# A 64x32 factorization of the row transform, with real and imaginary parts stacked on the partitions and unsummed filter products, in a spectral filter beside a gated linear unit

## The chip, the cores and the metric

The kernel runs on one core of a Trainium2 chip. The metric is device time in microseconds (us) of one execution; the profile's span, from a profiled execution, is some 2 us shorter. All runs quoted here are fast ones. Before took 206.78 us when the prediction was made (median of 3 runs, 206.33 to 206.89), and 206.92 to 206.98 in the three rounds of experiments (medians of 7 to 11 runs, 206.16 to 207.72).

## The reference

The output is the sum of the input, a two-dimensional spectral filter of its layer norm, and a gated product of the same layer norm.

```python
xn = (x - mean(x)) / sqrt(var(x) + 1e-5)             # x: 2048 x 640, bf16
X  = rfft2(xn, axes=(-2, -1))                        # 2048 x 321, complex
ya = irfft2(X * (w_r + 1j * w_i), s=(2048, 640))     # w_r, w_i: 2048 x 321
yb = ((xn @ w_gate) * (xn @ w_up)) @ w_down          # 640 x 1536, 1536 x 640
out = x + ya + yb
```

## The kernel before

A planner runs when the kernel is built. It knows every task, an estimated duration on each engine that may do it, and the buffers, and fixes the order of instructions on every engine. "First products" below means the matmuls with w_gate and w_up. The planner uses them, 512 columns wide, to fill TensorE while a spectral task waits for another engine.

The spectral stage goes through 16 iterations, each a chain over engines: column transform D (TensorE), its copy out of PSUM (ScalarE or VectorE), row transform C (TensorE), filter product WM (VectorE), sums CB (GpSimd), negations NG (ScalarE), inverse transform IA (TensorE). The planner keeps several iterations in flight. The filter rows come by one transfer for each of two halves of 64 partitions, w_r and w_i apart.

```python
for t in range(16):
    for w_ in range(2):                       # w_r, w_i
        for h in range(2):                    # two halves of 64 partitions
            dma(v_w[64 * h:64 * h + 64, wr, w_, 0:321], wvs[w_][:, k2, :])
    # D: 5 matmuls, real and imaginary columns side by side
    for k in range(5):
        n = 128 if k < 4 else 130
        matmul(psum[:, ...k * 128 + n], v_uq[:, k, t, :], v_fd[:, k * 128: k * 128 + n])
    # C: complex product as 4 real matmuls for two row groups
    matmul(ps[:, bk, 0:_LP],     v_tf[:, t, 0, :], a_r, start=True,  stop=False)
    matmul(ps[:, bk + 1, 0:_LP], v_tf[:, t, 0, :], a_i, start=True,  stop=False)
    matmul(ps[:, bk, 0:_LP],     v_tf[:, t, 1, :], a_i, start=False, stop=True)
    matmul(ps[:, bk + 1, 0:_LP], v_tf[:, t, 2, :], a_r, start=False, stop=True)
    # WM (VectorE): four products x * w.  ... CB (GpSimd): their sums, NG (ScalarE): negated copies ...
    # IA: 5 pairs of 128 columns; weights l1, l2 are read with a step of 4 for k < 4
    for k in range(5):
        matmul(dst, l1, v_ti[:, t, 0, :], start=True,  stop=False)
        matmul(dst, l2, v_ti[:, t, 1, :], start=False, stop=True)
```

## Time and profile before

| | before |
|---|---|
| time, span | 206.78 us, 204.3 us |
| TensorE busy | 98%, granted clock 1.00 throughout |
| VectorE, ScalarE, GpSimd busy | 87%, 59%, 11% |
| spacing of matmuls from start to start | 216 ns (512 columns), 137 (320 or 321), 56 (128) |
| first real product starts at | 7.57 us |

How to read it: TensorE has work from beginning to end, so the sum of its matmuls is the time, nearly. The other engines and the transfers count only where they let TensorE run dry. The prediction shows the views that carry this. One view is added here because the result turns on it: busy time in the stretch from 84 to 141 us, which is the spectral stage (columns: stretch, length, busy time of PE, PEld, DVE, ACT and POOL with instruction counts, granted clock, mean busy share of the 16 DMA engines, GB/s).

```profile
84.00:141.00 57.00, 56.30 (x478) 36.35 (x486) 44.95 (x144) 48.82 (x126) 21.56 (x32) 1.00 0.30 67
```

TensorE is idle for 0.7 of 57 us here, and the transfers bring 67 GB/s without anyone waiting for them.

### The profile page before, as it was taken

What the parts mean: (1) busy time and instruction counts of PE and PEld (TensorE: products, weight loads), DVE (VectorE), ACT (ScalarE), POOL (GpSimd) and SP (SyncE); (2) the same over time, 40 slices, a digit from 0 to 9 for tenths busy, and PEclk for the clock granted to TensorE, in tenths of its full rate; (3) what the DMA queues carried; (4) which work ended last, traced back from release to release, by engine and by line L of the source; (5) the groups of instructions that cost most, each with busy time, mean ns of one, the idle gap of its engine ahead of it and who ended that gap; (6) DMA issues with size and microseconds to landing.
All of it is one profiled execution on the core that took longest, in us unless ns stands there. A gap on an engine that the chain in (4) does not pass through costs nothing.

```text
span 204.3 us, 4499 instructions
## 1 busy us (share of the span) xinstructions
PE 199.7 (98%) x1681; PEld 137.2 (67%) x1695; DVE 178.7 (87%) x508; ACT 121.4 (59%) x282; POOL 21.8 (11%) x36
## 2 busy tenths in 40 slices
PE   7999999999999999999999999999999999999995
PEld 7998999554545455465777666666777787777774
DVE  3798999999999999949997997818999999999973
ACT  2379998999976577577999899878420222000000
POOL 0000000000000000003655365310000000000000
PEclk9999999999999999999999999999999999999999
DMA  6999993603139460001333343225033122324212
GB/s 179 301 342 383 387 210 15 67 0 64 32 66 242 86 202 0 3 0 27 66 65 60 68 113 65 65 70 158 0 98 113 55 76 83 112 80 111 83 35 62
DMA packets 30740, 21.69 MB, mean 106 GB/s; under 512 B 10752, under 2 KB 29696, under 8 KB 30592
## 3 DMA queue, kind: packets, MB, share of 16 engines
q1 hardware_dynamic: 29920, 21.06, 40.6%
q10 hardware_dynamic: 800, 0.36, 0.6%
q8 instruction: 13, 0.21, 0.4%
q14 instruction: 7, 0.06, 0.1%
HBM read 16.82 MB, written 2.62 MB: 95 GB/s over the span
## 4 chain that ended last, share of the span: by engine, by line
PE 92%; DVE 6%; issue 1%; ACT 1%
PE ps L969 36%; PE ps L1229 26%; PE ps L989 13%; DVE arena L1070 3%; PE ps L747 3%; PE ps L930 2%; PE ps L1146 2%; PE ps L1239 2%; PE ps L1034 2%; PE ps L1117 2%; PE ps L1118 2%; DVE arena L1073 1%; PE ps L1058 1%; PE ps L1055 1%; PE ps L1057 1%; PE ps L1056 1%
## 5 line engine op out<-in xcount | busy, mean ns | idle before, releaser
L719 ACT ACTIVATE arena<-ps 128x512 bf16<-128x512 f32 (+5 forms) x183 | 97.1, 568 | 48.7 <-PE ps L1146 23.4
L969 PE MATMUL ps<-arena 128*128 128x512 bf16 x346 | 80.1, 379 | 0.9 <-DVE arena L1073 0.3
L969 PEld LDWEIGHTS ps<-arena 128*128 128x128 bf16 x360 | 33.9, 98 | 36.5 <-ACT arena L719 0.8
L1229 PE MATMUL ps<-arena 128*128 128x320 bf16 (+2 forms) x396 | 56.7, 295 | 0.0
L1229 PEld LDWEIGHTS ps<-arena 128*128 128x128 bf16 x396 | 38.0, 98 | 13.9
L989 PE MATMUL ps<-arena 128*128 128x128 bf16 (+1 forms) x360 | 28.2, 237 | 0.1
L989 PEld LDWEIGHTS ps<-arena 128*128 128x128 bf16 x360 | 24.9, 98 | 2.5 <-ACT arena L719 0.7
L1070 DVE TENSOR_TENSOR arena<-ps,arena 128x256 f32<-128x256 f32 x64 | 22.6, 414 | 1.4 <-PE ps L1058 1.2
L1005 DVE TENSOR_TENSOR arena<-arena 128x512 bf16<-128x512 bf16 x36 | 15.3, 425 | 9.0 <-ACT arena L719 8.8
L1093 POOL TENSOR_TENSOR arena<-arena 128x256 bf16<-128x256 f32 x16 | 10.3, 644 | 111.5 <-DVE arena L1086 111.5
L1249 DVE TENSOR_TENSOR arena<-ps,arena 128x320 bf16<-128x320 f32 (+2 forms) x33 | 15.3, 473 | 3.8 <-PE ps L1239 3.8
L1094 POOL TENSOR_TENSOR arena<-arena 128x256 bf16<-128x256 f32 x16 | 11.9, 745 | 0.0
L1117 PE MATMUL ps<-arena 128*128 128x128 bf16 x80 | 10.4, 219 | 0.1
L1118 PE MATMUL ps<-arena 128*128 128x128 bf16 x80 | 10.4, 219 | 0.0
L1117 PEld LDWEIGHTS ps<-arena 128*128 128x128 bf16 x80 | 8.7, 111 | 1.7
L1118 PEld LDWEIGHTS ps<-arena 128*128 128x128 bf16 x80 | 8.7, 112 | 1.4
L1239 PE MATMUL ps<-arena 128*128 128x320 bf16 (+2 forms) x33 | 9.1, 295 | 0.0
L883 DVE TENSOR_TENSOR arena<-arena 128x384 f32<-128x384 bf16 x16 | 8.8, 551 | 0.0
L773 ACT ACTIVATE arena<-arena 128x640 bf16<-128x640 bf16 x10 | 8.3, 825 | 0.0
L782 DVE BATCH_NORM_STATS2 arena<-arena 128x6 f32<-128x320 bf16 x12 | 5.4, 481 | 2.8 <-DMA arena<-in_A_x_dram 2.7
L767 ACT ACTIVATE arena<-arena 128x640 bf16<-128x640 bf16 x10 | 7.3, 734 | 0.3 <-DMA arena<-in_A_x_dram 0.2
L1073 DVE TENSOR_TENSOR arena<-ps,arena 128x260 f32<-128x260 f32 x16 | 7.0, 438 | 0.0
(72 smaller groups left out, 235.7 us busy)
## 6 DMA issues: line engine op xcount, KB each, us to landing
arena<-in_A_x_dram SPq DMA_DIRECT2D x20, 160.0 KB, 2.5
out_dram<-arena SPq DMA_DIRECT2D x31, 80.0 KB, 1.6
arena<-c_tf SPq DMA_DIRECT2D x4, 384.0 KB, 11.2
arena<-in_A_w_r_dram SPq DMA_DIRECT2D x32, 40.1 KB, 2.3
arena<-in_A_w_i_dram SPq DMA_DIRECT2D x32, 40.1 KB, 2.3
arena<-in_B_w_gate_dram SPq DMA_DIRECT2D x4, 320.0 KB, 5.4
arena<-in_A_x_dram SPq DMA_DIRECT2D x1, 1280.0 KB, 10.3
arena<-c_ti SPq DMA_DIRECT2D x2, 512.0 KB, 4.9
```

What stands on the lines that cost most here:

```text
L719: return c.e.activation(dst, src, _ACTF.Copy)
L969: ins = c.e.matmul(ps[:, bk, :], v_gw[:, w, j, ft, :], v_xt[:, j, rows], start=(j == 0), stop=(j == 4))
L989: ins = c.e.matmul(ps[:, bk, w * n:(w + 1) * n], v_gw[:, w, j, ft, :], v_xt[:, j, rows], start=(j == 0), stop=(j == 4))
L1005: return c.e.tensor_tensor(v_ht[:, ft0, rows], v_gbf[:, rr, 0, :], v_gbf[:, rr, 1, :], _OP.mult)
L1070: c.e.tensor_tensor(v_p[:, ar, w, :, 128 * h:128 * h + 128].rearrange("p c (m k) -> p c m k", k=4), xh.rearrange("p c (m k) -> p c m k", k ...
L1093: c.e.tensor_tensor(v_y[ar][:, 512:768], p01[:, 0:256], p10[:, 0:256], _OP.add)
L1094: return c.e.tensor_tensor(v_y[ar][:, 256:512], p00[:, 0:256], p11[:, 0:256], _OP.subtract)
L1117: c.e.matmul(dst, l1, v_ti[:, t, 0, :], start=True, stop=False)
L1118: ins = c.e.matmul(dst, l2, v_ti[:, t, 1, :], start=False, stop=True)
L1229: ins = c.e.matmul(ps[:, bk, 0:sl3.stop - sl3.start], v_ht[:, ft, a * 128:(a + 1) * 128], v_wd[:, ft, sl3], start=(ft == 7 and px is None) ...
L1239: return c.e.matmul(ps[:, bank_of(own), 0:sl3.stop - sl3.start], v_sm[:, 2, :], v_v[:, a, sl3], start=False, stop=True)
L1249: return c.e.tensor_tensor(v_out[:, a % 2, sl3], ps[:, bk, 0:sl3.stop - sl3.start], v_xr[:, xs, sl3], _OP.add)
```

## The change

The intent is to save TensorE work. With the length of 2048 factored as 64 by 32, one row group has 32 points; its real and imaginary parts together fill 64 partitions, and the two sets that C multiplies fill 128. The complex product becomes one real matmul for each row group. The filter product is no longer summed: IA gets the products with w_r and with w_i as they are, and its matmul adds them up, since they lie on different partitions or in its second weight. CB falls away; a larger negation remains, on GpSimd. The filter rows are needed on four blocks of 32 partitions, two of them equal and two in reverse order of row groups, and are loaded for two iterations at once.

```diff
-_R = 32
+_R = 64
 # filter loads, one set for every two iterations, two slots
-dma(v_w[64 * h:64 * h + 64, wr, w_, 0:321], wvs[w_][:, k2, :])
+parts = [(dw[0:64], wv[:, q0:q0 + _WQ, :].rearrange("k1 q l -> k1 (q l)").unsqueeze(0).to_broadcast(
+    [2, _S1, _WQ * 321]), 64 * _WQ * 642)]
+for d_ in range(2):
+    parts.append((dw[64 + 32 * d_:96 + 32 * d_, ...], wv[:, _R - q0 - o_:_R - q0 - _WQ:-1, :], ...))
 # D: 10 matmuls of 64 or 65 columns for 5 of 128 or 130
+for w in range(2):
+    matmul(ps[:, bk + w, k * 64:k * 64 + n], v_uq[:, k, t, :], v_fd[:, k * 128 + w * n: ...])
 # C: 1 matmul for each of two row groups, for 4 in all
+for g in range(2):
+    matmul(ps[:, bk + g, 0:_LP], v_tf[:, 2 * t + g, :], v_a[:, ar, 324 * g:324 * g + _LP])
 # NG: on GpSimd, planned at 1.6 us
+tensor_scalar(yg[:, :, 0:256], yg[:, :, 512:768], -1.0, None, mult)
+tensor_copy(yg[:, :, 833:896], yg[:, :, 1025:1088])
+tensor_scalar(yg[:, :, 896:961], yg[:, :, 1024:1089], -1.0, None, mult)
+tensor_copy(yg[:, :, 961:1024], yg[:, :, 769:832])
 # IA: 20 matmuls of 64 columns for 10 of 128, output in runs of four floats
+matmul(dst[:, g], l1, v_ti[:, 2 * t + g, 0, :], start=True,  stop=False)
+matmul(dst[:, g], l2, v_ti[:, 2 * t + g, 1, :], start=False, stop=True)
 # ... tables of constants, PSUM copies, and an order retuned by the planner's parameters: cut
```

## The prediction

> **What bounds the kernel now.** I read the page's busy shares first, then the chain that ended last, then busy time by stage, then the order of matmuls inside the changed stage, and last the first nine microseconds.
>
> ```profile
> PE 199.7 (98%) x1681; PEld 137.2 (67%) x1695; DVE 178.7 (87%) x508; ACT 121.4 (59%) x282; POOL 21.8 (11%) x36
> ...
> PE 92%; DVE 6%; issue 1%; ACT 1%
> ```
>
> The first line is busy time by engine, the second the chain's shares. "Busy" for matmuls proves little, since each is drawn with its latency. So I took start-to-start spacings from the trace: 216 ns for 512 columns, 137 ns for 320 or 321, 56 ns for 128, 107 ns for 128 in the first 5 us, before the clock rises. Summed over the program's own counts (a few records are missing) they give about 200 us of the 204.3 us span. From the tenth microsecond to the last matmul I find only one real gap, 0.2 us at 118.5 us. TensorE runs out of work nowhere, and only a shorter sum of spacings, or an earlier start, can shorten the kernel. By stage (head, first products, row transforms, spectral stage, end):
>
> ```profile
> 0.00:7.60 7.60, 6.55 (x68) 6.51 (x69) 3.41 (x12) 1.87 (x3) 0.20 (x4) 1.00 0.80 219
> 7.60:36.30 28.70, 28.50 (x389) 25.96 (x388) 27.36 (x95) 25.02 (x66) 0.00 (x0) 1.00 0.97 265
> 36.30:89.00 52.70, 52.38 (x289) 26.05 (x294) 49.42 (x135) 39.75 (x79) 0.00 (x0) 1.00 0.35 74
> 89.00:142.00 53.00, 52.36 (x455) 34.22 (x462) 42.62 (x138) 46.50 (x122) 21.56 (x32) 1.00 0.32 73
> ```
>
> Columns: stretch, length, busy PE, weight loads, DVE, ACT, POOL. In the spectral stage (fourth row) DVE is busy 80% and ACT 88%: near limits, not limits. In the row stage (third row) DVE is at 94%, the closest second.
>
> **What the Trainium skill says.** "TensorE: Matmul & The Clock Gate", section "Back-to-back issue gap", gives N/2.4 + 2.5 ns for a warm stream and a floor of about 25 ns; for real streams with a weight load each it gives 81 ns at 128 columns. The trace agrees with the formula (56, 137, 216) and not with 81. No matmul of before is narrower than 128, so 64 columns, by the formula an estimate of 29.2 ns, is untested here.
>
> The same page, "Weight-path perf modes", says that full 128-column bf16 loads use a fast path that reads weights 32 bits at a time. After a wait, the trace starts a second load 15 ns behind the first, so a load is much shorter than its drawn 98 ns. But the inverse transform's weights are read with a step of four elements, and those loads are longer:
>
> ```profile
> L989 PEld LDWEIGHTS ps<-arena 128*128 128x128 bf16 x360 | 24.9, 98 | 2.5 <-ACT arena L719 0.7
> ...
> L1117 PEld LDWEIGHTS ps<-arena 128*128 128x128 bf16 x80 | 8.7, 111 | 1.7
> ```
>
> The means are 98 and 111 ns; single stepped loads show up to 117. If the 13 to 19 ns are real occupancy, a stepped load takes some 15 + 15 = 30 ns (estimate): hidden under 56 ns, just not under 29.
>
> "ScalarE: Activation LUTs", section "What ACT_TABLE_LOAD costs", states about 1283 ns for the load of a function table, again at each switch of set. The trace has one such load, 1.28 us (below).
>
> "PSUM — Partial Sum Buffer", section "Specifications (TRN2)", warns that non-contiguous access slows matmuls. The new inverse matmuls write runs of four floats, every second run. No such write is in the trace of before.
>
> **The change part by part.** It touches the column transform D, the row transform C, the filter product, the helper parts, the inverse IA; then a retuned order.
>
> TensorE. Before, D has 80 matmuls of 128 to 130 columns, C 64 of 321, IA 160 of 128: 80 x 56 + 64 x 137 + 160 x 56 ns = 4.5 + 8.8 + 9.0 = 22.2 us. After, stacking real and imaginary parts on partitions makes C one matmul per row group instead of four for two: 32 of 321 = 4.4 us. D becomes 160 of 64 or 65, IA 320 of 64: the columns streamed stay the same and the instructions double. At 29.2 ns that is 4.7 + 9.3 us. New sum 18.4 us, a gain of 3.8 us. If the 256 stepped loads hold IA at 32 ns, it costs 256 x 2.8 = 0.7 us of it, so 3.1 us are left.
>
> VectorE. Per pair of row groups, four products of 256 and one of 260 stay four of 256 and become two of 130 (by the trace's slope near 0.22 us each, for 0.36); the two subtractions of 65 (0.14 each) go. So 1.97 us becomes 1.76, 16 times: 3.3 us less. But the evacuation of D becomes four copies of 64 partitions x 321 (about 0.37 us on ACT, 0.42 on DVE, estimates from 256 and 512) for 0.86 before, and the instruction order gives 20 of the 64 to DVE: +8.3 us against some 1.7 before. DVE is up by about 3 us in the stage.
>
> ScalarE. It loses the negations (0.9 us x 16 = 14.4) and gains evacuation, 44 x 0.37 = 16.3 us for 14 x 0.8 = 11. Lighter by some 9 us.
>
> GpSimd. It swaps two f32 additions (1.37 us) for one negation of 512 elements and three pieces of 126 or 130, bf16. I guess 1.6 to 2.2 us per pair, under the 2.9 us of TensorE work per pair in the new order. None of these three lies on the path if the order holds: between a C and its IA the new order puts 4.7 to 6 us of other matmuls, and product (1.8), negation (2.2) and hand-overs (0.5) need 4.5.
>
> Head. Before:
>
> ```profile
> 1.05 5.30 PE L747 MATMUL ps<-arena 128*128 128x128 bf16 x48 [1.05 <-DVE arena L754]
> 1.70 1.28 ACT L808 ACT_TABLE_LOAD   x1 [1.70 <-PEq L1328]
> ...
> 4.59 0.21 ACT L808 ACTIVATE arena<-arena 128x1 bf16<-128x1 bf16 x1 [1.62 <-DVE arena L804]
> ...
> 5.03 0.39 DVE L826 TENSOR_SCALAR arena<-arena 128x640 bf16<-128x640 bf16 x1
> ```
>
> The first normalised tile is ready at 5.42, the warm-up ends at 6.15, the transpose follows and the first real product starts at 7.57. The change cuts 8 warm-up matmuls (0.86 us), which seems to allow 0.65 us. But it also sends tile 1's statistics to ScalarE ahead of tile 0's square root, and the built program then has two table loads: one before the first statistics pass, one before the root. The second tile lands at 3.91; 0.85 us of statistics and 1.28 of loading put the root at 6.1 for 4.59, the scaled tile at 6.9, the transpose after it, and the first product, behind VectorE's longer list, near 8.4: +0.85. Tile 1 then follows sooner (two waits of 0.42 us together, at 9.2 and 10.3, fall away). Net +0.4 us. TensorE also idles from 5.3 to 6.9, which could delay the rise of the clock: up to +0.8 more.
>
> Row stage. D now comes 7 us of TensorE work sooner (more first products are moved behind it) and DVE has only 4.7 us less to do before it. By sums of durations the last row result and the matmul that wants it are within some 0.6 us. I allow 0.5 us of stalls here and in the spectral stage.
>
> Sum: -3.8 + 0.7 + 0.4 + 0.5 = -2.2 us, 204.6; half a microsecond back for the retuned order, which was presumably measured: 204.2.
>
> **Rivals.** (1) Everything hides: 29.2 ns holds, no second load in the way, no stalls: -3.8 - 0.65 = -4.4, 202.4 us. For it: TensorE has hidden every load so far. Against: the stepped loads and the table load. (2) Narrow matmuls cost as much as wide ones, because each carries a 128-column load: 480 x 56 = 26.9 us in place of 14.0, +12.9, so about 216 us. The 15 ns between loads speaks strongly against; the unseen strided PSUM write leaves room for a part of it, say 40 ns in IA, +3.5 us. (3) VectorE or GpSimd becomes the bound of the spectral stage: DVE's list from first to last product sums to 39.5 us against 43.2 us of TensorE work, so it fits by 9% only; a GpSimd negation over 2.9 us would add (excess) x 16, for instance 3 us at 3.1.
>
> **Range and chances.** Faster by over 2% means under 202.64, which needs rival 1 nearly whole: 0.17. Slower by over 2% means over 210.9: rival 2 or a strong rival 3: 0.07. Between them 0.76. Range 202.0 to 207.2, wide to the slow side for the IA spacing, the clock and the stalls.
>
> **What would show it.** C's spacing unchanged at 137 ns with half the matmuls; D's near 29 ns; IA's 29 to 33 (over 40: rival 2 in part). A second table load around 4.8 to 6.1 us and the first product at about 8.4, not under 7. VectorE and GpSimd waits ahead of IA in the chain of waits would mean rival 3. The prediction is wrong low if gaps over 0.2 us appear before the row or inverse matmuls, and wrong high if the head starts sooner than in before and TensorE shows no gap.

## The result

The changed kernel took **228.69 us** (median of 4 runs, 226.57 to 229.67) against 206.76 of before in the same rounds: a ratio of 1.105, 95% interval 1.096 to 1.114. Slower by 10.5%, far outside the range.

The page of after, busy time, then TensorE and its granted clock in 40 slices of 5.7 us (tenths), then the chain's shares:

```profile
PE 206.1 (90%) x1900; PEld 138.8 (61%) x1917; DVE 177.3 (78%) x500; ACT 126.9 (56%) x261; POOL 40.5 (18%) x68
...
PE   7799999999999997299769579959999999999995
...
PEclk9999999999999999589979979997999999999999
...
PE 45%; DVE 22%; DMA 17%; SPq 10%; ACT 2%; issue 2%
```

TensorE, busy 98% before, is at 90%. The holes lie in slices 16 to 27, the spectral stage, and in five of the slices from 17 to 28 the clock falls to between 5 and 8 tenths, where before had none below 9. The chain, 92% TensorE before, is now 17% DMA.

Who waited for whom (engine and line that waited, what released it, us in total, times, the longest):

```profile
PEld ps L1068 <- DMA arena<-in_A_w_i_dram: 15.2, 4, 5.6
PE ps L1068 <- DMA arena<-in_A_w_i_dram: 14.0, 4, 5.1
```

L1068 is the row transform C. Four times it stands waiting for the filter load, 14.0 us in all. It waits although it reads no filter. The filter product WM frees the PSUM banks that C fills, and the planner lets C take them only once everything else that this product needs is there. So C inherits the wait for the filter.

The windows of after, with two that lie wholly inside such waits:

```profile
84.00:100.00 16.00, 10.80 (x77) 5.50 (x78) 9.54 (x27) 7.51 (x17) 7.17 (x11) 0.79 0.41 121
100.00:120.00 20.00, 16.76 (x209) 10.93 (x211) 11.56 (x34) 14.25 (x28) 9.70 (x17) 0.91 0.32 86
120.00:141.00 21.00, 16.28 (x187) 10.05 (x190) 12.38 (x38) 13.73 (x29) 11.23 (x19) 0.92 0.32 89
141.00:160.00 19.00, 16.25 (x170) 9.32 (x172) 11.59 (x35) 10.87 (x21) 12.03 (x20) 0.91 0.14 36
...
90.50:94.50 4.00, 0.00 (x0) 0.00 (x0) 2.51 (x9) 0.22 (x1) 3.47 (x5) 0.71 0.36 121
...
129.50:131.00 1.50, 0.00 (x0) 0.00 (x0) 0.06 (x1) 0.00 (x0) 1.50 (x3) 1.00 0.13 50
```

Two readings. First, the clock column: each wait is followed by stretches at half clock. Weighted by length, what is missing from full clock in these 76 us is 0.21 x 16 + 0.09 x 20 + 0.08 x 21 + 0.09 x 19 = 8.6 us, that is, 17.1 us at half clock. But 3.2 of these 17.1 us fall into the waits themselves, where TensorE has nothing to do (the row from 90.5 us shows it: no matmul, clock 0.71). TensorE worked at half clock for 13.8 us, and that took some 6.9 us more than at full clock, on top of the waits. Second, the last row: while TensorE does nothing but wait for a transfer, the 16 DMA engines are busy for 13%, two sixteenths, and move 50 GB/s. The trace has 64 packets of 2568 bytes for each load with the broadcast source, of about 104 ns each, and in this stretch 9 or 10 of them start every half microsecond. Two engines carry the whole load: 64 x 104 / 2 = 3.3 us for 160.5 KB, and w_r and w_i take 6.7 us for two iterations, whose D, C and IA and the first products planned between them hold TensorE for only 5.8.

Three smaller things are in the groups of after (line, engine, operation, shapes, count, busy us, mean ns, idle before):

```profile
L1103 POOL TENSOR_SCALAR arena<-arena 128x512 bf16<-128x512 bf16 x16 | 24.1, 1507 | 119.4 <-DVE arena L1089 119.4
...
L1122 PEld LDWEIGHTS ps<-arena 128*128 128x128 bf16 x160 | 12.8, 118 | 4.1 <-ACT arena L715 1.9
```

The large negation takes 1.5 us, and with its three small pieces GpSimd is busy for 40.5 / 16 = 2.53 us an iteration where the plan has 1.6. The weight loads of IA are drawn with 118 ns where IA of before had 111; from start to start its stepped matmuls are some 34.5 ns apart (33 to 38), those with contiguous weights 29.

The start of after, in order of time (start, length, engine, line):

```profile
5.14 1.28 ACT L804 ACT_TABLE_LOAD   x1
6.43 0.21 ACT L804 ACTIVATE arena<-arena 128x1 bf16<-128x1 bf16 x1
...
7.40 0.69 PE L840 MATMUL ps<-arena 128*128 128x128 bf16 x5 [1.91 <-DVE arena L822]
...
9.82 0.68 PE L988 MATMUL ps<-arena 128*128 128x128 bf16 x6
```

The second table load is where the prediction put it, and TensorE stands idle for 1.91 us ahead of its first transpose. The first real product starts at 9.82 us. The 36 filling matmuls between run at half clock, 53 ns each.

### The profile page after: what moved, and what is told of

Read it like the earlier page. It is cut to its first block, busy times and chain, and to the rows that moved or that the text cites. A ratio compares the mean times of both kernels' runs of the same rounds, so it can differ in the third digit from the quotient of the medians. Undisturbed runs are those within 1.5% of the kernel's fastest.

```text
span 227.9 us, 4935 instructions
## 1 busy us (share of the span) xinstructions
PE 206.1 (90%) x1900; PEld 138.8 (61%) x1917; DVE 177.3 (78%) x500; ACT 126.9 (56%) x261; POOL 40.5 (18%) x68
## 4 chain that ended last, share of the span: by engine, by line
PE 45%; DVE 22%; DMA 17%; SPq 10%; ACT 2%; issue 2%
PE ps L1234 23%; DMA arena<-in_A_w_i_dram 16%; SPq L709 10%; PE ps L968 8%; PE ps L988 5%; DVE arena L882 2%; DVE arena L1004 2%; PE ps L1244 2%; DVE arena L1086 2%; DVE arena L893 2%; DVE arena L883 1%; PE ps L1068 1%; PE ps L1151 1%; DMA arena<-in_A_x_dram 1%; DVE arena L1005 1%
## 5 line engine op out<-in xcount | busy, mean ns | idle before, releaser
L715 ACT ACTIVATE arena<-ps 128x512 bf16<-128x512 f32 (+5 forms) x203 | 106.9, 561 | 67.9 <-PE ps L968 30.2
L968 PEld LDWEIGHTS ps<-arena 128*128 128x128 bf16 x360 | 34.9, 101 | 39.7 <-issue 5.5
L1234 PE MATMUL ps<-arena 128*128 128x320 bf16 (+2 forms) x396 | 55.8, 295 | 0.0
L1234 PEld LDWEIGHTS ps<-arena 128*128 128x128 bf16 x396 | 37.7, 98 | 13.9 <-DVE arena L1254 0.3
L1103 POOL TENSOR_SCALAR arena<-arena 128x512 bf16<-128x512 bf16 x16 | 24.1, 1507 | 119.4 <-DVE arena L1089 119.4
L1086 DVE TENSOR_TENSOR arena<-ps,arena 128x256 bf16<-128x256 f32 x64 | 24.0, 418 | 20.1 <-PE ps L1068 20.1
L988 PEld LDWEIGHTS ps<-arena 128*128 128x128 bf16 x360 | 25.3, 98 | 1.7
L1068 PE MATMUL ps<-arena 128*128 128x321 bf16 x32 | 7.1, 316 | 14.0 <-DMA arena<-in_A_w_i_dram 14.0
L1122 PEld LDWEIGHTS ps<-arena 128*128 128x128 bf16 x160 | 12.8, 118 | 4.1 <-ACT arena L715 1.9
L1122 PE MATMUL ps<-arena 128*128 128x64 bf16 x160 | 13.7, 203 | 1.0 <-ACT arena L715 0.7
L1123 PE MATMUL ps<-arena 128*128 128x64 bf16 x160 | 13.6, 204 | 0.0
L1123 PEld LDWEIGHTS ps<-arena 128*128 128x128 bf16 x160 | 12.1, 118 | 1.6 <-issue 0.6
L1068 PEld LDWEIGHTS ps<-arena 128*128 128x128 bf16 x32 | 2.3, 101 | 16.0 <-DMA arena<-in_A_w_i_dram 15.2
L716 DVE CAST arena<-ps 64x321 bf16<-64x321 f32 x20 | 9.8, 492 | 0.6 <-PE ps L1045 0.3
L1089 DVE TENSOR_TENSOR arena<-ps,arena 128x130 bf16<-128x130 f32 x32 | 9.3, 291 | 0.0
L1105 POOL TENSOR_SCALAR arena<-arena 128x130 bf16<-128x130 bf16 x16 | 9.1, 568 | 0.0
## 6 DMA issues: line engine op xcount, KB each, us to landing
arena<-in_A_w_r_dram SPq DMA_DIRECT2D x8, 160.5 KB
arena<-in_A_w_i_dram SPq DMA_DIRECT2D x8, 160.5 KB
arena<-in_A_w_r_dram SPq DMA_DIRECT2D x14, 80.2 KB
arena<-in_A_w_i_dram SPq DMA_DIRECT2D x14, 80.2 KB
```

The source lines that it names most:

```text
L715: return c.e.activation(dst, src, _ACTF.Copy)
L968: ins = c.e.matmul(ps[:, bk, :], v_gw[:, w, j, ft, :], v_xt[:, j, rows], start=(j == 0), stop=(j == 4))
L988: ins = c.e.matmul(ps[:, bk, w * n:(w + 1) * n], v_gw[:, w, j, ft, :], v_xt[:, j, rows], start=(j == 0), stop=(j == 4))
L1086: c.e.tensor_tensor(dst, xh.unsqueeze(1).to_broadcast([128, 2, 32, 4]), wv, _OP.mult)
L1103: c.e.tensor_scalar(yg[:, :, 0:256], yg[:, :, 512:768], -1.0, None, _OP.mult)
L1122: c.e.matmul(dst, l1, v_ti[:, 2 * t + g, 0, :], start=True, stop=False)
```

## The experiments

Nine kernels ran on the chip, all compared with before on the same chip. The main theory is A: the broadcast source confines the filter loads to two DMA engines. R blames the size of the ring of filter slots (two slots of two iterations) instead, P the negation on GpSimd.

| run | time, us (median) | ratio to before, 95% interval |
|---|---|---|
| after (the change) | 228.69 | 1.105 (1.096 to 1.114) |
| a1_split: plain loads | 210.75 | 1.019 (1.014 to 1.024) |
| a2_sqrt: and one table load | 209.12 | 1.009 (1.007 to 1.011) |
| b1_bcast: before with broadcast loads | 222.16 | 1.072 (1.069 to 1.076) |
| r1_finer: after with a finer ring | 220.76 | 1.066 (1.061 to 1.071) |
| c2_short: a2 with a shorter negation | 206.82 | 0.999 (0.993 to 1.004) |
| c1_plan: a2, true negation time planned | 209.26 | 1.011 (1.007 to 1.015) |
| c3_dve: a2, negation on VectorE | 214.22 | 1.034 (1.030 to 1.038) |
| c4_half: a2, negation split VectorE/GpSimd | 211.17 | 1.021 (1.017 to 1.025) |
| d1_best: a2, negation split, replanned | 205.65 | 0.993 (0.991 to 0.995) |

### a1_split: the same bytes without the broadcast

```diff
-parts = [(dw[0:64], src.unsqueeze(0).to_broadcast([2, 32, 1284]))]
+parts = [([dw[0:32], dw[32:64]], [src, src])]     # two transfers of 32 partitions, same task
```

The order of the instructions of all compute engines is unchanged.

> The changed kernel, same order of instructions on every engine that computes; only each filter load whose source is a broadcast with outer dimension 2 is issued as two plain loads of 32 partitions. Theory A (such a load runs on two of the 16 DMA engines, 64 packets of 2568 bytes at 104 ns on 2 engines = 3.3 us, 6.7 us per group of two iterations that need only 5.8 us of TensorE work): C's waits for the filter load fall from 14 us to under 0.5, packets of 2568 bytes go from 20 per us to over 60, no half-clock stretch after the first 10 us, time 205 to 208 (before 206.8; -3.8 for the matmuls counted, +1.4 for inverse matmuls at 34.5 ns instead of 29, +1.8 for the later head). Rival R (a ring of two slots, reloaded too late, whatever engines carry it): over 4 us of C's waits stay, 214 or more. Rival P (GpSimd's negation, 2.5 us an iteration for 1.6 planned): waits of the inverse matmuls for GpSimd appear instead, 210 or more.

Measured 210.75 us: the broadcast alone cost 18 us. The time is above theory A's range, so A is the largest part and not all; it is where rival P put it (210 or more). C's waits for the filter load are gone from the table of waits, and the clock shows 1.00; the window of the stage, to be set beside the one of before:

```profile
84.00:141.00 57.00, 53.27 (x630) 32.27 (x639) 44.64 (x131) 45.92 (x90) 39.47 (x62) 1.00 0.33 83
```

The issues of the broadcast loads (how many, KB each; the page of after gives no landing time for them), and then all filter loads of a1_split with the us from issue to landing:

```profile
arena<-in_A_w_r_dram SPq DMA_DIRECT2D x8, 160.5 KB
arena<-in_A_w_i_dram SPq DMA_DIRECT2D x8, 160.5 KB
```

```profile
arena<-in_A_w_r_dram SPq DMA_DIRECT2D x30, 80.2 KB, 2.4
arena<-in_A_w_i_dram SPq DMA_DIRECT2D x30, 80.2 KB, 2.5
```

Each load of 160.5 KB is now two of 80.2 KB, which makes 16 of the 30 in each row; they land in some 2.4 us. Of the packets of 2568 bytes, up to 58 start in one microsecond, where after never had more than 20 in the stage (theory A expected over 60).

### b1_bcast: the reverse, in the kernel before

```diff
-dma(v_w[64 * h:64 * h + 64, wr, w_, 0:321], wvs[w_][:, k2, :])
+dma(v_w[64 * h:64 * h + 64, wr, w_, 0:321],
+    wvs[w_][0:32, k2, :].unsqueeze(0).to_broadcast([2, 32, 321]))   # wrong result on purpose
```

> The kernel before with every filter load's source written as a broadcast of 32 rows with outer dimension 2 (same bytes, same number of loads, wrong result on purpose). Theory A: 64 packets of 642 bytes at 33 ns on 2 engines = 1.06 us a load, 4.2 us an iteration for 2.9 of TensorE work: 216 to 226 us, with waits for the filter load and half-clock stretches as in the changed kernel. If the broadcast itself costs nothing and the new structure is to blame: 206.8 within 1%.

Measured 222.16 us. The result is wrong (relative error 0.028). Nothing of the factorization is in this kernel, and the same wait appears, at its row transform:

```profile
PE ps L1056 <- DMA arena<-in_A_w_i_dram: 9.6, 7, 2.7
```

So the form of the load is enough to slow before by 7%, and taking it away is enough to free after: A holds from both sides.

### r1_finer: the ring of filter slots

```diff
-_NW = 2; _WQ = 4      # two slots, each of four row groups (two iterations)
+_NW = 4; _WQ = 2      # four slots, each of two row groups; broadcast source kept
```

> The changed kernel with the broadcast loads kept, but the ring of the same size cut into four slots of one iteration instead of two of two, so a slot's reload starts after one iteration. Rival R (late triggers): most of C's waits go, 210 or less. Theory A: two engines still have 2 x 32 packets of 1284 bytes x 2 loads an iteration, some 3.6 us for 2.9 of TensorE work: over 4 us of waits for the filter load stay, 215 or more.

Measured 220.76 us, 8 us better than after, and still 10 us behind a1_split. The waits are more frequent and shorter:

```profile
PE ps L1068 <- DMA arena<-in_A_w_i_dram: 10.6, 8, 1.8
```

Waits of at most 1.8 us in place of 5.1, and no half clock after them: from 84 to 160 us the granted clock is 1.00. (The mean of 0.992, for after's 0.963, comes from one stretch in the head, 7.4 to 10.8 us.) So part of the 18 us was the price of long waits, which the clock then charges again; but the ring isn't the cause.

### a2_sqrt: one table load

```diff
+if b == 1:                                              # ahead of ScalarE's first statistics pass
+    activation(scratch[:, 0:1], v_dum[:, 0:1], Sqrt)    # loads the set with the square root first
```

> a1_split and one tiny square root ahead of ScalarE's first statistics pass, so that the first function table loaded is the one with the root in it. Theory H (the second table load sits in the head's path): one table load instead of two, the first transpose at about 6.1 us for 7.40, first real product about 1.3 us sooner than in a1_split (9.8), time 1 to 2 us under a1_split. Rival: the head is hidden by loads of the weights: within 0.4 us of a1_split.

Measured 209.12 us, 1.6 less than a1_split. One table load is left, at 1.73 us, and the first real product starts at 7.00 us, 0.57 before that of the kernel before:

```profile
1.73 1.28 ACT L770 ACT_TABLE_LOAD   x1 [1.73 <-DVE arena L733]
...
7.00 0.72 PE L996 MATMUL ps<-arena 128*128 128x128 bf16 x10
```

In a1_split it started at 8.60 us (the 9.8 of the expectation was after's), so it comes 1.60 us sooner, and the kernel gains about that.

### c2_short: a shorter negation in the same order

a2_sqrt's span is 207.0 us, 2.7 above before's 204.3. In 13 of its 16 iterations IA's first matmul starts 0.06 to 0.20 us after GpSimd's last instruction of the same iteration (in 11 of them 0.14 to 0.20). What the spacings of matmuls exceed the usual ones by, most of it ahead of IA, adds up to some 5.6 us from 84 us to the end of the stage at 142 us (0.2 in before). The wait table puts three of IA's waits, 2.1 us, down to a ScalarE copy. These copies end 0.06 to 0.07 us before IA starts, and GpSimd's last instruction 0.14 to 0.15 us before it, so the trace alone does not tell which one IA waits for.

```diff
-tensor_scalar(yg[:, :, 0:256], yg[:, :, 512:768], -1.0, None, mult)
+n_ = 256 if t < 3 else 64                               # wrong result on purpose
+tensor_scalar(yg[:, :, 0:n_], yg[:, :, 512:512 + n_], -1.0, None, mult)
```

> a2_sqrt with GpSimd's large negation cut from 2x256 to 2x64 columns in iterations 3 to 15 (wrong result on purpose); the order of instructions on every engine is the same as in a2_sqrt, and the plan is the same. In a2_sqrt GpSimd took 2.55 us an iteration where the plan reckoned with 1.6, and in 13 of 16 iterations the inverse transform's first matmul started 0.14 to 0.20 us after the negation's end. From the two tensor_scalar sizes there (1507 ns at 512, 568 at 130) the cut piece should take about 0.57 us, so an iteration's negation some 1.7 us, near the plan. Theory P (the negation gates the inverse transform and makes the some 5.7 us of TensorE stalls that a2_sqrt has between 84 and 141 us): 204 to 206.5 us, the waits ahead of the inverse transform under 2 us in all. Rival Q (ScalarE's copies or the DMA queues gate it, the negation only ends at the same time): 208.3 to 209.5, as a2_sqrt's 209.1.

Measured 206.82 us, 2.3 less than a2_sqrt with the order unchanged. The columns left out keep an older iteration's values, so the result is wrong by construction; the comparison with the reference passed even so, its tolerance being wider than this error. The group of IA in a2_sqrt, then in c2_short:

```profile
L1130 PE MATMUL ps<-arena 128*128 128x64 bf16 x160 | 12.9, 197 | 2.8 <-ACT arena L721 2.1 <-POOL arena L1114 0.7
```

```profile
L1131 PE MATMUL ps<-arena 128*128 128x64 bf16 x160 | 12.8, 197 | 0.5 <-POOL arena L1115 0.5
```

Idle time ahead of IA falls from 2.8 to 0.5 us, the ScalarE entry vanishing with it, though nothing was done to ScalarE. The first of the three IA (111.87 us in a2_sqrt, where the copy ended at 111.80) now starts at 111.34 us, while the same copy ends only at 112.14: IA does not need it. Theory P stands as the second cause, though the time is just above its range (206.5 at most): some waits moved to C, 0.8 us for a filter load and 0.3 more.

### c1_plan, c3_dve, c4_half: moving the negation

```diff
 # c1_plan: the planner is told the measured time
-"pool": 1600.0
+"pool": 2550.0
 # c3_dve: the whole negation on VectorE
-engines ("pool", "act")
+engines ("dve",), planned at 600 ns
 # c4_half: the large piece on VectorE, the three small ones on GpSimd, at once
+T("NB", "dve", 250.0): tensor_scalar(yg[:, :, 0:256], yg[:, :, 512:768], -1.0, None, mult)
```

> a2_sqrt with one number changed: the planner is told that GpSimd's negation takes 2.55 us instead of 1.6. It then gives 6 of the 16 negations to ScalarE and orders the inverse transforms later. Theory P: most of the stalls go, 205 to 207 us. If ScalarE, which is busy for some 45 of the 57 us of the stage, becomes the bound with the six negations: 208 or more. Rival Q: no change, 208.3 to 209.5.

> a2_sqrt with the negation on VectorE (planned at 0.6 us). Theory P with cheap bf16 copies on VectorE: 204 to 206.5 us. Rival 3 of the prediction in its other form (VectorE becomes the bound of the stage: it is busy for some 44 of 57 us there and gets 16 times 0.6 to 1.0 us more): 208 to 212 us, with waits of the column transform or the inverse transform for VectorE.

> a2_sqrt with the negation split: the large piece on VectorE, the three small ones stay on GpSimd (some 1.15 us in a2_sqrt), at the same time. Theory P: the wait of the inverse transform for the negation falls from 2.55 us to about 1.2 after the filter product, 204 to 206.5 us. If VectorE and GpSimd slow each other down when they work at once, the small pieces take more than 1.15 us in all and the gain is smaller: 206.5 to 208.5. Rival Q: 208.3 to 209.5.

Measured 209.26, 214.22 and 211.17 us: three misses of theory P's numbers, none better than a2_sqrt. By the numbers alone c1_plan falls into rival Q's range (and that of ScalarE as the bound, 208 or more), and c3_dve and c4_half lie above every range given. (In c1_plan ScalarE got seven of the sixteen negations, not six as the expectation says.) The negation itself did become short in c3_dve:

```profile
L1111 DVE TENSOR_SCALAR arena<-arena 128x512 bf16<-128x512 bf16 x16 | 4.7, 293 | 0.3
```

293 ns for the large piece and about 193 for each small one, 0.87 us in place of 2.55. Why, then, slower? Each of these edits made the planner choose another order. The table compares when the last first product, TensorE's filling work, starts, and when the last matmul of IA starts:

| | last first product, us | last IA, us | difference |
|---|---|---|---|
| before | 141.7 | 136.4 | -5.3 |
| a2_sqrt | 142.5 | 141.6 | -0.9 |
| c2_short | 140.7 | 139.8 | -0.9 |
| c1_plan | 137.4 | 140.8 | 3.4 |
| c4_half | 137.1 | 142.6 | 5.6 |
| c3_dve | 135.3 | 145.6 | 10.3 |
| d1_best | 141.2 | 138.4 | -2.8 |

In the three misses the filling work is used up before the last iterations are through, and TensorE then sees the bare chain of the last iterations over four engines. The difference orders the three times. In c3_dve the gaps there are 0.4 to 1.9 us long, and the clock falls with them:

```profile
PEclk9999999999999999999999999975799999999999
```

That this is the reason is read from the traces of these three and from the next run, which changes the order on purpose; no run changes the supply of filling work alone. In c4_half the small copy that starts together with VectorE's negation took 424 ns for 297 in a2_sqrt; what slowed it was not tested by itself.

### d1_best: a version that beats both

```diff
-NG on GpSimd, planned 1600 ns
+negation of row group 0 on GpSimd (2.47 ns a column + 250), of row group 1 on ScalarE or VectorE,
+small pieces on GpSimd (1200 ns); 32 ns planned for each IA matmul
-caps["a"] = 2        # pairs of PSUM banks for spectral tasks
+caps["a"] = 3
```

> A candidate for the best kernel: a2_sqrt with the negation's large piece split between engines (group 0's 256 columns on GpSimd, group 1's on ScalarE or VectorE, whichever the planner finds free), the small pieces on GpSimd, the durations measured so far given to the planner (GpSimd 2.47 ns a column + 250, small pieces 1.2 us, 32 ns for each matmul of the inverse transform) and three bank pairs instead of two for the spectral tasks. If the filter loads and the negation were the whole cause (theories A and P), this reaches what the matmul count leaves: 204 to 206 us, faster than before by 0.5 to 1.5%, with under 3 us of waits ahead of the inverse transform and at the end of the stage. If a third cause limits the stage, it stays at 206.5 or more.

Measured 205.65 us over 6 runs (204.95 to 205.87) with a correct result, inside the expected range: 0.7% faster than before (a small gain, but its interval leaves out 1) and 10% faster than after. From its page, TensorE's busy share and clock:

```profile
PE 197.5 (97%) x1900; PEld 135.8 (67%) x1917; DVE 179.2 (88%) x505; ACT 128.6 (63%) x272; POOL 30.6 (15%) x68
...
PEclk9999999999999999999999999999999999999999
```

The filling work lasts 2.8 us past the last IA again, and no idle time is left ahead of IA's first matmuls. What remains in the stage are 1.6 us of waits of C. The run changes the split, the planned durations and the bank pairs together, so its 3.5 us against a2_sqrt are not divided among them.

## Why the prediction was wrong

**The step that failed** is the sentence "None of these three lies on the path if the order holds". It lists VectorE, ScalarE and GpSimd, and no transfer. The prediction costs every compute instruction that the change adds, and has no term for the filter loads, which the change rewrote as well; its list of what the change touches leaves them out. Its own sign for being wrong low, gaps over 0.2 us ahead of the row matmuls, came true. The form of these loads decides: a source with a leading dimension of two ran on two of sixteen DMA engines. a1_split takes 18 us off by splitting them, b1_bcast puts 15 us on before by the same form alone.

This could have been read beforehand. The Trainium skill, "DMA: Bandwidth & Descriptors", section "Rules for kernel authors", says that an outermost dimension smaller than 16, for instance "a leading zero-stride broadcast of c copies", confines a whole transfer to at most c engines. The trace agrees: share 0.13 = 2/16, 50 GB/s. With the durations of before, 642-byte packets of 33 ns, one could have estimated some 2568 / 642 x 33 = 132 ns for a packet of the new size, (64 x 132 / 2) x 2 = 8.4 us for two iterations against 5.8 us of TensorE work: a wait, though not its exact size.

**The clock** was in the prediction only for the head. In the spectral stage it took 6.9 us, half as much as the 14.0 us of waits ahead of it. "TensorE: Matmul & The Clock Gate", section "HAM oscillation — how this bites in real kernels", describes just this: a wait for a transfer that crosses the window of the activity monitor throttles TensorE, and the work after it starts slow. The trace agrees in kind, with half clock after each of the four waits. It does not agree with the figure that the section gives, idle time over some 3.4 us: two of the four waits are shorter, 2.9 us and 1.9 us (the latter 0.8 us after one of 0.7), while r1_finer's eight of at most 1.8 us left the clock alone. That makes a long wait dearer than the same time in short ones, which fits r1_finer.

**Rival 3** held for GpSimd as a second cause, at a lower threshold than the prediction gave it. It asked whether the negation exceeds 2.9 us, the TensorE work of an iteration: that is throughput. The prediction also had a sum for one iteration's way from C to IA, 1.8 + 2.2 + 0.5 = 4.5 us under 4.7 to 6 us of other matmuls. This step failed too: the negation measured 2.53 us, not at most 2.2, and where several C follow each other closely, their negations queue up on GpSimd. In a2_sqrt IA starts 4.9 to 8.9 us after its C. So TensorE waits at places that the plan fixed on the belief in 1.6 us, although GpSimd is busy for only 40.4 of the 57 us from 84 to 141. c2_short gives 2.3 us for it. The allowance of 0.5 us for stalls was the mis-sized term: a2_sqrt has some 5.6.

**The matmul arithmetic was right** and rival 2 fell. C keeps 137 ns with half the matmuls, D runs at 28 to 30 ns for a predicted 29.2, IA with contiguous weights at 29. (The section that the prediction cites gives its formula for an isolated matmul; here streams with a weight load each follow it.) One size was off: stepped weights hold IA at 34.5 ns, so the term is 256 x 5.3 = +1.4 us instead of +0.7. The kernel does gain 3.8 - 1.4 = 2.4 us of TensorE time.

**The head**: the mechanism was right, a second table load that delays the first square root, and so was its size: in a1_split, whose head is the same program, the first product came at 8.60 us for a predicted 8.4. That it came at 9.82 in the profiled run of after is the prediction's hedge about the clock, at 1.2 us instead of up to 0.8. There TensorE was at half clock until 10.22 us and its 36 filling matmuls took 1.9 us; in a1_split they ran at 29 ns each and took 1.0. When the clock rises differs from trace to trace (6.75 us in before, 3.75 in a2_sqrt), and no run tests why. The one table load of a2_sqrt takes 1.6 us off.

**VectorE and ScalarE.** VectorE was to be busier by 3 us in the stage and ScalarE to be relieved of 9. From 84 to 141 us a2_sqrt has VectorE at 44.0 us for 45.0 and ScalarE at 45.5 for 48.8. So VectorE was not busier there, and ScalarE was relieved of about a third of what was predicted; the window does not hold exactly the same work in both kernels, and no run ties a loss to either.

**The sum.** For after: -3.8 (matmuls) + 1.4 (stepped weights) + 14.0 (waits) + 6.9 (clock) + 2.3 (head: 9.82 for 7.57) = 20.8 us of the 23.6 by which the span grew from 204.3 to 227.9; the other 2.8 are not divided, the waits of IA for the negation among them. For a2_sqrt: -3.8 + 1.4 - 0.57 + 5.6 - 0.2 (before's own stalls) = 2.4 us of its span's excess of 2.7 (207.0 for 204.3). A slip in the prediction's own sum matters little: 204.6 less half a microsecond is 204.1, not 204.2.

## What to carry to other kernels

Cost the transfers that a change rewrites as carefully as its instructions: outermost dimension, packets, engines that can share them, and the time that TensorE leaves for them. Where an order is fixed by a plan, an engine need not be the bound to cost time; it is enough that it is slower than the plan believed, so measure each planned duration first and check that filling work lasts to the end of the last chain. When TensorE is the bound, look at its clock beside its waits, since in after the four waits of 1.9 to 5.1 us cost half as much again in clock.

## What the Trainium skill lacked or had wrong

- "GPSIMD Engine Reference", section "Engine selection", calls one-input elementwise work on GpSimd roughly line-rate. Here a bf16 multiplication by a constant took 1514 ns at 512 columns and 579 at 130 (a2_sqrt): (1514 - 579) / 382 = 2.45 ns a column and some 260 ns fixed. VectorE did the same 512 columns in 293 ns.
- "TensorE: Matmul & The Clock Gate", section "Weight-path perf modes — Fast Weight Load (FWL) and DoubleRow", takes stepped weights for the fast path and gives no price. Here loads with a step of four elements were drawn with 118 ns for 98 and held 64-column matmuls 34.5 ns apart, for 29 with contiguous weights.
- "PSUM — Partial Sum Buffer", section "Specifications (TRN2)", warns that non-contiguous access slows matmuls. IA's output in runs of four floats kept 29 ns wherever its weights were contiguous, so no cost of it shows.
- "ScalarE: Activation LUTs", section "What ACT_TABLE_LOAD costs", adds about 1380 ns of draining to a load's 1283. In after ScalarE's instruction ahead of the load ended at 5.12 us, the load ran from 5.14 to 6.42 and the next activation started at 6.43, so no such draining shows.
